# Blocks 3 to 5 in 64-token chunks, q scaled while it is turned, y copied by two engines, and a new order of the work

## The chip, the cores and the metric

One core of one Trainium2 chip runs the whole program. The metric is the device time of one execution in microseconds (us), the median of several runs; lower is better. Engines are named as in the profile: PE is TensorE (matmuls; PEld its weight loads), DVE is VectorE, ACT is ScalarE, POOL is GpSimd, SP is SyncE. PSUM has eight banks, numbered 0 to 7.

## The reference

Two layers follow each other: a retention with a decay per head, then a channel mix.

```python
# B=4, H=8, S=768, D=64
for t in range(S):
    state = gamma[h] * state + outer(k[:, :, t], v[:, :, t])
    y[:, :, t] = (1 / sqrt(D)) * q[:, :, t] @ state
x = y.transpose(0, 2, 1, 3).reshape(B, S, 512)
xk = mu_k * x + (1 - mu_k) * x_prev        # x_prev: x one token earlier
xr = mu_r * x + (1 - mu_r) * x_prev
k = relu(xk @ w_k)                          # 512 -> 1024
out = sigmoid(xr @ w_r) * (k * k @ w_v)     # 512 x 512, 1024 -> 512
```

## The kernel before, in words

The tokens are cut into twelve blocks of 256, three for each batch element; block n holds tokens of batch n // 3. The recurrence is done in chunks: within a chunk the scores of q and k are multiplied by a causal mask and then by v, and what went before comes in through a 64x64 state for each head, which is summed from chunk to chunk. The decay is taken out of the scores by scaling: v is multiplied by powers of gamma when it is cast (`vs`), and y by the opposite powers when it leaves PSUM (`gy`).

A block can take one of three forms. Blocks 6 to 11 (`HALF`) use chunks of 64 tokens and matmuls of 64x64 tiles. Blocks 2 to 5 (`WIDE`) use chunks of 128 tokens, with wider tiles. Blocks 0 and 1 use 128-token chunks in four quarters. `PAIRQ` and `PAIRK` name the blocks whose q or k is laid out so that two heads are turned (transposed) by one 128x128 product; the others in `HALF` are turned in 64x64 quarters. Blocks 9 to 11 are turned by DMA.

After its y is in `xT`, a block goes through the channel mix: the difference to the token before (`dx`), xk and xr (`X`), the product with w_k (`K`), relu and square, the product with w_r (`R`), the sigmoid, the product with w_v (`V`), the product of both and the store. Blocks 3 and 4, 6 and 7, 9 and 10 share `dx`, `X` and `K`.

Nothing is scheduled by a compiler: the string `ORDER` lists every step, and each engine gets its instructions in that order. A word such as `K.2.0@3` is a code, its arguments (block, part) and the PSUM banks; `~a`, `~v`, `~p`, `~s` choose ScalarE, VectorE, GpSimd's queue or SyncE's queue. The codes used below are:

- `lq`, `lk`, `lv`: loads of a block, issued by POOL; `st`: store of a result, by SP; `tq`, `tk`: turn of q or k by DMA, by SP
- `Tq`, `Tk`: turn by PE into PSUM; `Eq`, `Ek`: the copy of it to `qT`, `kT` by ACT
- `vs`: v scaled and cast, by DVE; `S`: scores (PE); `M`: mask (DVE, PSUM to `a`)
- `C`: k times v, the state of each chunk (PE); `U`: its running sum (DVE or ACT, into `tg`, at the end `t`); `G`: the decay to the next block, into `tg`
- `I`: the part of y from the states that goes to the other chunk half (PE, first into y's two banks); `Y`: scores times v, and in `HALF` blocks also the rest of the state part; `J`: that rest in `WIDE` blocks; `D`: y from PSUM to `xT`
- `dx`, `X`, `K`, `Qa` (relu, into `kr`), `Qb` (square, into `k2s`), `R`, `s` (sigmoid, into `rs`), `V`, `O` (the result, `os`)
- `z`: matmuls on zeros, early in the program

Rings of buffers bind the order: four each for q, k, v as loaded and for `kr`, three each for `vs`, `qT`, `kT` and `a`.

Of the kernel before, what the change touches and what calls it, by code (L numbers as in the profile page):

```python
# [37 lines left out]
z.2@5 Y.1 lv.2~p X.0.0.1 X.0.0.2 z.1@5 K.0.2@4 Tk.2@5 D.1~v X.0.1.0 dx.1~v Qa.0.2 X.0.1.2
X.1.0.0 Ek.2~a K.0.3@0 Qa.0.3 Qb.0.3 X.1.0.2 X.1.0.1 S.2.1@67 K.0.0@5 Qa.0.0 K.0.1@0 X.1.0.3
K.1.2@1 K.1.0@5 Qb.0.0 wr~p X.1.1.0 Qa.0.1 U.1.1 G.1~a vs.2~v X.0.1.3 Qa.1.0 Qa.1.2 Qb.0.1  # L40
X.1.1.1 C.2@0 U.2.0 K.1.1@3 Qa.1.1 I.2@45 lv.3~p M.2.1~v S.2.0@01 K.1.3@2 lq.3~p Qb.1.2 R.0.1@3
Qa.1.3 lk.3~p M.2.0~v X.1.1.2 Y.2 lk.4~p lq.4~p Qb.1.3 s.0.1 lv.4~p X.1.1.3 vs.3~v J.2 D.2~v
R.1.0@2 R.1.1@3 Qb.1.1 s.1.0 Tq.3@2 s.1.1 Eq.3~a C.3@67 Tk.3@4 Ek.3~a R.0.0@3 s.0.0 Tk.4@2
S.3.0@01 wv.0~p dx.2~v X.2.0.0 X.2.0.2 X.2.0.1 X.2.0.3 X.2.1.1 S.3.1@45 Ek.4~a K.2.0@3 lq.7~p
Tq.4@2 M.3.1~v U.3.0~a U.3.1 Qa.2.0 wv.1~p Eq.4~a K.2.3@6 Qa.2.3 M.3.0~v K.2.1@7 S.4.1@45
S.4.0@23 vs.4~v M.4.0~v K.2.2@6 Qb.0.2 I.3@01 Y.3 C.4@23 G.3~a M.4.1~v U.4.0 lk.5~p Qb.1.0
Qa.2.2 V.1.0.0@6 lq.5~p I.4@45 Qa.2.1 Qb.2.1 X.2.1.3 J.3 D.3~v Y.4 V.0.1.0@7 V.0.0.0@0 J.4 U.4.1
Tq.7@23 Eq.7~a V.1.1.0@1 V.1.1.1 G.4~a Qb.2.0 dx.3~v V.0.0.1 Tk.5@2 Ek.5~a D.4~v dx.4~v V.0.1.1
Qb.2.3 V.1.0.1 Tq.5@2 X.3.0.3 X.3.0.1 X.3.0.2 Eq.5~a X.3.0.0 K.3.1@3 Qa.3.1 K.3.3@4 O.1.1 O.0.0
S.5.0@01 O.1.0 O.0.1 lv.5~p lq.6~p M.5.0~v S.5.1@23 vs.5~v K.3.2@5 Qa.3.3 lk.6~p Qb.3.3 K.3.5@4  # L50
M.5.1~v X.2.1.0 Qa.3.2 X.2.1.2 Tq.6@67 Qa.3.5 Tk.6@01 Eq.6~a lv.6~p lv.7~p Ek.6~a C.5@5 U.5.0
X.3.1.0 Qb.3.1 K.3.0@4 Qa.3.0 lk.7~p K.3.7@6 S.6@23 Qb.3.2 M.6~v I.5@01 Y.5 vs.6~v V.2.1.0@7
R.2.1@2 lv.10~p Qb.2.2 Qa.3.7 K.3.4@6 st.0.0 vs.7~v Qb.3.7 s.2.1 st.0.1 V.2.1.1 Tk.7@45 Qb.3.5
Qa.3.4 X.3.1.3 X.3.1.1 Qb.3.0 C.6@23 st.1.0 J.5 Ek.7~a X.3.1.2 R.2.0@6 lv.8~p U.6.0~a D.5~v
U.6.1 U.6.2 U.6.3 V.2.0.0@4 s.2.0 K.3.6@6 dx.5~v Qa.3.6 lq.8~p lk.8~p st.1.1 R.4.1@5 I.6@01
# [24 lines left out]
R.11.1@0 V.11.0.0@7 R.11.0@4 O.9.0 st.9.0 V.11.0.1 O.10.1 s.11.1 st.10.1 s.11.0 O.10.0 st.10.0  # L80
O.11.0 st.11.0 Vc.11.1.0@4 Oc.11.1.0 sc.11.1.0~s Vc.11.1.1@6 Oc.11.1.1 sc.11.1.1~a
"""


# [1 line left out]
def kernel(  # L86
# [210 lines left out]
    def trans(a):
        def go(e, n, j0=0, j1=NJ):
            src = held_as(n, a)
            pt = turned(n, a, j0, j1)  # L300
            for j in range(j0, j1):
                for i in range(2):
                    if quarters(n, a):
                        for u in range(2):
                            for s, h, hp in heads(j):
                                nc.tensor.transpose(  # L306
                                    pt[low(s), u, j - j0, i], src[low(u), i, h], ident[low(u), low(u)]
                                )
                        continue
# [256 lines left out]

    def yout(e, n, u=None):
        x, c = col(n)
        if half(n):
            x = x[:, :, c : c + TM].rearrange("p j (i u t) -> p j i u t", i=2, u=2)  # L570
            g = gy.rearrange("p j (i u t) -> p j i u t", i=2, u=2)
            for v in range(2):
                nc.vector.tensor_tensor(
                    out=x[:, :, :, v],
                    in0=banks("I", n)[:, v].rearrange("p (j i t) -> p j i t", j=NJ, i=2),
                    in1=g[:, :, :, v], op=ALU.mult,
                )
            return
# [88 lines left out]
        nc.scalar.activation(out=kr, in_=banks("K", n, g, *u), func=AF.Relu)  # L667
# [143 lines left out]
    def load_wv(e, h):  # L811
# [62 lines left out]
```

## Time and profile before

| | us |
|---|---|
| median of 3 runs | 154.3 |
| lowest and highest run | 154.3, 154.64 |
| span of the profiled execution | 152.4 |
| PE busy | 145.3 |
| DVE busy | 128.0 |
| ACT busy | 94.5 |
| POOL busy | 62.1 |

The span runs from the first to the last instruction of the profiled execution; a run's time also has what lies around it, here 1.9 us between the span and the median. Busy shares are of the span: 95% for PE, 84% for DVE, 62% for ACT. The granted clock of PE was 1.0 throughout. PE's busy time alone does not say that PE is at its peak, since matmuls are pipelined; so the places where it waits, and the start times of its groups, are what is read.

### The profile page before, as it was taken

The numbers are of one execution on the slowest core, as the hardware profiler recorded it, in microseconds if no ns is written. First come the engines' busy times: TensorE is split into PE (matmuls) and PEld (weight loads), VectorE is DVE, ScalarE is ACT, GpSimd is POOL, SyncE is SP. The second block draws the span as 40 slices with busy tenths as digits, with TensorE's granted clock in tenths as the row PEclk, the third lists the DMA queues.
The fourth block names the chain that finished last, engine by engine and source line by source line (L and its number), as shares of the span: only waits on it lengthen the run. The fifth ranks groups of instructions, "written<-read, shape, count | busy, mean of one in ns | idle before, by whom it ended". The sixth has DMA issues, their size and how long they took to land.

```text
span 152.4 us, 4956 instructions
## 1 busy us (share of the span) xinstructions
PE 145.3 (95%) x2129; PEld 82.4 (54%) x2129; DVE 128.0 (84%) x204; ACT 94.5 (62%) x172; POOL 62.1 (41%) x77
## 2 busy tenths in 40 slices
PE   7969899999999999999999999999999999999991
PEld 3345467657864545545448544447664444466460
DVE  2289999999999999999999998998999999331651
ACT  3655259979955679966418807869450089739430
POOL 7965658999746920599989000000000000000000
PEclk9999999999999999999999999999999999999999
DMA  5999999999999999299999999928103013003153
GB/s 146 237 241 192 181 240 237 148 148 223 167 178 216 213 225 286 68 239 166 258 188 238 236 168 126 152 89 109 38 4 138 0 71 142 0 0 138 69 207 138
DMA packets 56525, 23.83 MB, mean 156 GB/s; under 512 B 48056, under 2 KB 52024, under 8 KB 56504
## 3 DMA queue, kind: packets, MB, share of 16 engines
q0 software_dynamic: 45200, 14.95, 82.1%
q1 hardware_dynamic: 10872, 8.26, 22.3%
q8 instruction: 16, 0.26, 0.7%
q10 hardware_dynamic: 432, 0.32, 0.7%
q14 instruction: 5, 0.04, 0.1%
HBM read 24.31 MB, written 6.29 MB: 201 GB/s over the span
## 4 chain that ended last, share of the span: by engine, by line
PE 73%; DVE 11%; DMA 11%; issue 2%; ACT 0%; DVEq 0%; POOLq 0%
PE ps L700 24%; PE ps L688 14%; PE ps L635 12%; PE ps L645 11%; DMA kT<-k 6%; DMA v<-in_v_dram 5%; DVE a L420 3%; PE ps L507 2%; PE ps L311 2%; DVE xk L621 2%; DVE xT L580 2%; DVE dx L595 2%; PE ps L544 1%; DVE vs L280 1%; PE ps L388 1%
## 5 line engine op out<-in xcount | busy, mean ns | idle before, releaser
L700 PE MATMUL ps<-wv,k2s 128*128 128x512 f16 x184 | 43.9, 380 | 0.0
L667 ACT ACTIVATE kr<-ps 128x512 f32<-128x512 f32 x48 | 27.9, 594 | 23.0 <-PE ps L635 14.9
L700 PEld LDWEIGHTS <-k2s 128*128 128x128 f16 x184 | 17.2, 98 | 19.0
L706 DVE SCALAR_TENSOR_TENSOR os<-ps,rs 128x512 f32<-128x512 f32 x23 | 15.2, 684 | 12.1 <-PE ps L700 6.5
L688 PE MATMUL ps<-wr,xr 128*128 128x512 f16 x96 | 24.0, 379 | 0.0
L259 POOL DMA_DIRECT2D v<-in_v_dram x20 | 18.0, 911 | 13.6 <-DVE vs L280 8.3
L645 PE MATMUL ps<-xk,wk 128*128 128x256 f16 x192 | 23.4, 273 | 0.0
L635 PE MATMUL ps<-xk,wk 128*128 128x512 f16 x96 | 22.8, 379 | 0.0
L420 DVE TENSOR_TENSOR a<-ps,c_sb 128x1024 f16<-128x1024 f32 (+1 forms) x20 | 21.9, 1110 | 0.0
L694 ACT ACTIVATE rs<-ps 128x512 f32<-128x512 f32 x24 | 14.3, 594 | 10.6 <-PE ps L688 8.8
L645 PEld LDWEIGHTS <-wk 128*128 128x128 f16 x192 | 18.2, 98 | 3.9
L621 DVE SCALAR_TENSOR_TENSOR xr<-dx,mu,xT 128x256 f16<-128x256 f32 (+1 forms) x36 | 19.3, 566 | 0.0
L621 DVE SCALAR_TENSOR_TENSOR xk<-dx,mu,xT 128x256 f16<-128x256 f32 (+1 forms) x36 | 18.9, 569 | 0.3
L259 POOL DMA_DIRECT2D k<-in_k_dram x20 | 17.7, 896 | 3.5 <-DMA wv<-in_moe_w_v_dram 1.6
L280 DVE TENSOR_TENSOR vs<-v,csm_sb 128x1024 f16<-128x1024 f32 x12 | 14.5, 1217 | 3.3 <-DMA v<-in_v_dram 3.3
L675 ACT ACTIVATE k2s<-kr 128x512 f16<-128x512 f32 x24 | 14.7, 626 | 0.4
L595 DVE TENSOR_TENSOR dx<-xT 128x1024 f32<-128x1024 f32 x12 | 14.6, 1221 | 0.2
L635 PEld LDWEIGHTS <-wk 128*128 128x128 f16 x96 | 9.1, 98 | 10.5 <-issue 0.2
L679 ACT ACTIVATE k2s<-kr 128x512 f16<-128x512 f32 x24 | 14.5, 625 | 0.3
L688 PEld LDWEIGHTS <-xr 128*128 128x128 f16 x96 | 9.0, 98 | 10.0
L265 ACT COPY qT<-ps 128x1024 f16<-128x1024 f16 (+1 forms) x10 | 9.2, 924 | 7.7 <-PE ps L317 3.7
L265 ACT COPY kT<-ps 128x1024 f16<-128x1024 f16 (+1 forms) x10 | 9.3, 934 | 6.9 <-PE ps L306 3.4
(73 smaller groups left out, 151.3 us busy)
## 6 DMA issues: line engine op xcount, KB each, us to landing
out_dram<-os SPq DMA_DIRECT2D x23, 256.0 KB, 3.8
v<-in_v_dram POOLq DMA_DIRECT2D x20, 256.0 KB, 6.8
k<-in_k_dram POOLq DMA_DIRECT2D x21, 128.0 KB, 6.9
q<-in_q_dram POOLq DMA_DIRECT2D x13, 128.0 KB, 7.1
q<-in_q_dram POOLq DMA_DIRECT2D x5, 256.0 KB, 9.0
v<-in_v_dram POOLq DMA_DIRECT2D x2, 512.0 KB, 7.3
wv<-in_moe_w_v_dram POOLq DMA_DIRECT2D x2, 512.0 KB, 9.5
wk<-in_moe_w_k_dram POOLq DMA_DIRECT2D x2, 256.0 KB, 9.6
```

The costliest lines, as they stand in the source:

```text
L259: e.dma_start(out=to[:, i, hs], in_=src[:, i])
L265: e.copy(out=out, in_=in_)
L280: e.tensor_tensor(out=VS(n), in0=V32(n).rearrange("p (h i d) -> p i h d", i=2, h=H), in1=gks[:, int(half(n) or wide(n)), :, :, None].to_br ...
L420: nc.vector.tensor_tensor(out=dst, in0=dst if n in SPLITM else src, in1=mask[:, None, None, :].to_broadcast(list(dst.shape)), op=ALU.mult,)
L595: e.tensor_tensor(out=DX(k)[:, :, m * TM + t0 : m * TM + t1], in0=x[:, :, c + t0 : c + t1], in1=x[:, :, c - 1 + t0 : c - 1 + t1], op=ALU.s ...
L621: nc.vector.scalar_tensor_tensor(out=XM[w](k)[:, j, t0:t1], in0=DX(k)[:, j, t0:t1], scalar=mu[:, w * NCO + j : w * NCO + j + 1], in1=x[:, ...
L635: nc.tensor.matmul(banks("K", n, g), lhsT=wk16[:, co, g * P : g * P + P], rhs=XM[0](k)[:, co, :], start=(co == 0), stop=(co == NCO - 1),)
L645: nc.tensor.matmul(pz[:, i, :], lhsT=wk16[:, co, fo * P : fo * P + P], rhs=XM[0](k)[:, co, m * TM + t0 : m * TM + t1], start=(i == 0 and c ...
L667: nc.scalar.activation(out=kr, in_=banks("K", n, g, *u), func=AF.Relu)
L688: nc.tensor.matmul(banks("R", n, tb), lhsT=XM[1](k)[:, co, t : t + P], rhs=wr16[:, co, :], start=(co == 0), stop=(co == NCO - 1),)
L700: nc.tensor.matmul(banks("V", n, tb), lhsT=K2(n)[:, fo, tb * P : tb * P + P], rhs=wv16[:, fo, :], start=(fo == 0), stop=(fo == NFO - 1),)
L706: nc.vector.scalar_tensor_tensor(out=OS(2 * n + tb), in0=banks("V", n, tb), scalar=1.0 / (KSC * KSC), in1=RS(2 * n + tb), op0=ALU.mult, op ...
```

## The change

The blocks 3, 4 and 5 leave `WIDE` and the pair layouts and join `HALF`: their q and k are turned in 64x64 quarters, and scores, states and y are computed in chunks of 64 tokens. That changes their instructions: one mask of 1024 columns in place of two, four running sums in place of two (three in place of one in block 5, whose last sum isn't needed).

For blocks 3 to 8 the turn of q is no longer a transposition by an identity but a product with a scaled identity, `turn`, which has the power of gamma for each token and head. Its result is float32 in two banks, where it was float16. Their y then needs one constant factor alone, so `D` becomes a scaled copy instead of a product with `gy`; it can run on ACT, and does for blocks 4, 6 and 8 (`D.4~a`, `D.6~a`, `D.8~a`). The scaled identity is built once by two DVE instructions (`tu`) from a small table `late` that SP loads (`ce`) into the tile `mu8`, after `mt` has read that tile; it lies in the unused half of the first `a` buffer.

A new step `sy` (`settle`) makes ACT read a few elements of y's banks after `I` and before `Y`, in blocks 2, 3, 4, 5, 7, 10 and 11. `Y` on PE then waits for that read. The two banks of each two-bank tile are neighbours. The whole `ORDER` is written anew.

```diff
-HALF = (6, 7, 8, 9, 10, 11)
+QDN = 64.0
+HALF = (3, 4, 5, 6, 7, 8, 9, 10, 11)
-PAIRQ = (3, 4, 5, 9, 10, 11)
-PAIRK = (3, 4, 5, 9, 10, 11)
-WIDE = (2, 3, 4, 5)
+PAIRQ = (9, 10, 11)
+PAIRK = (9, 10, 11)
+WIDE = (2,)
+QS = (3, 4, 5, 6, 7, 8)
...
-M.0.1.2.4~v I.0@01 mt@2 me lq.1~p S.0.0.2.4@67 M.0.0.2.4~v lq.2~p G.0~a
+I.0@01 mt@2 M.0.1.2.4 S.0.0.2.4@67 me ce~s G.0~a
...
+    late = mu8[:, 0 : 2 * H + W]
+    turn = A2(0)[:, 2 * H * W :].rearrange("p (i h t) -> p i h t", i=2, h=H)
...
+    def load_late(e):
+        e.dma_start(out=late, in_=lated.ap())
+    def scaled_eye(e, h0, h1):
+        hs = slice(h0, h1)
+        gq = late[:, 0 : 2 * H].rearrange("p (i h) -> p i h", i=2)
+        to = [P, 2, h1 - h0, W]
+        e.tensor_tensor(
+            out=turn[:, :, hs], in0=late[:, None, None, 2 * H :].to_broadcast(to),
+            in1=gq[:, :, hs, None].to_broadcast(to), op=ALU.mult,
+        )
...
+                                if scaled(n, a):
+                                    nc.tensor.matmul(
+                                        pt[low(s), u, j - j0, i], lhsT=src[low(u), i, h],
+                                        rhs=turn[low(u), i, h], start=(j == j0 and i == 0),
+                                        stop=(j == j1 - 1 and i == 1), skip_group_check=True,
+                                    )
+                                    continue
...
+    def settle(e, n):
+        if wide(n):
+            u = slice(1 if first(n) else 0, 2)
+            copy(e, seen_y[:, u], banks("I", n)[:, u, 0 : NJ * C : C])
+        else:
+            copy(e, seen_y[low(0), 0, 0:2], banks("I", n)[low(0), 0, NJ * C - 2 :])
...
+        if n in QS:
+            x = x[:, :, c : c + TM].rearrange("p j (i u t) -> p u j i t", i=2, u=2)
+            y = banks("I", n).rearrange("p u (j i t) -> p u j i t", j=NJ, i=2)
+            for v in range(2):
+                if e is nc.scalar:
+                    e.activation(
+                        out=x[:, v], in_=y[:, v], func=AF.Copy, scale=0.125 * KSC / KUP * QDN
+                    )
+                else:
+                    e.tensor_scalar(
+                        out=x[:, v], in0=y[:, v], scalar1=0.125 * KSC / KUP * QDN, scalar2=None,
+                        op0=ALU.mult,
+                    )
+            return
```

Three places in the order of instructions follow. The first is on VectorE, early in the program: from y of block 0 (`xT` from `ps`) over its `dx` and first `X` (`xk`, `xr`) to the sum and the masks of block 1. Before:

```order
L580 TENSOR_TENSOR xT_130<-ps,gy_sb 128x2x4x128
L595 TENSOR_TENSOR dx_99<-xT_130 128x4x256
L621 SCALAR_TENSOR_TENSOR xk_101<-dx_99,mu,xT_130 128x256
L621 SCALAR_TENSOR_TENSOR xr_104<-dx_99,mu,xT_130 128x256
L485 TENSOR_TENSOR tg_1_94<-ps,tg_1_88 128x256
L420 TENSOR_TENSOR a_1_84<-ps,c_sb 128x1024 x2
L621 SCALAR_TENSOR_TENSOR xk_101<-dx_99,mu,xT_130 128x256 x3
```

And now:

```order
L640 TENSOR_TENSOR xT_130<-ps,gy_sb 128x2x4x128
L655 TENSOR_TENSOR dx_99<-xT_130 128x4x256
L681 SCALAR_TENSOR_TENSOR xk_101<-dx_99,mu,xT_130 128x256
L310 TENSOR_TENSOR a_0_83<-mu_124 128x2x256 x2
L681 SCALAR_TENSOR_TENSOR xr_104<-dx_99,mu,xT_130 128x256
L522 TENSOR_TENSOR tg_1_94<-ps,tg_1_88 128x256
L457 TENSOR_TENSOR a_1_84<-ps,c_sb 128x1024 x2
L681 SCALAR_TENSOR_TENSOR xk_101<-dx_99,mu,xT_130 128x256 x3
```

The two instructions that build `turn` (written into `a_0` from the tile of mu) have come between two `X`; the rest stands as before.

The second place is on ScalarE around the decay of block 3 (`G.3`, four instructions into `tg_1_88`), with the copies of q (`qT`), relus (`kr`), squares (`k2s`) and a sigmoid (`rs`) ahead of it. Before:

```order
L265 CAST tg_0_93<-ps 128x256
L667 ACTIVATE kr_109<-ps 128x512
L265 COPY qT_78<-ps 128x1024
L667 ACTIVATE kr_110<-ps 128x512
L679 ACTIVATE k2s<-kr_107 128x512
L490 ACTIVATE tg_1_88<-t_0_86,csm_sb 128x64 x4
L679 ACTIVATE k2s<-kr_108 128x512
```

And now:

```order
L276 CAST qT_78<-ps 128x2x4x128
L745 ACTIVATE k2s<-kr_108 128x512
L276 CAST tg_0_90<-ps 128x256
L745 ACTIVATE k2s<-kr_109 128x512
L760 ACTIVATE rs_112<-ps 128x512
L727 ACTIVATE kr_110<-ps 128x512
L727 ACTIVATE kr_107<-ps 128x512
L727 ACTIVATE kr_108<-ps 128x512
L527 ACTIVATE tg_1_88<-t_0_86,csm_sb 128x64 x4
L276 COPY seen_y<-ps 64x2
```

The read `sy.3` (`seen_y`) stands behind `G.3`, and more relus stand ahead of `G.3` than before.

The third place is on SyncE's queue, where the turns by DMA for blocks 9 to 11 stand among the stores. Before:

```order
L713 DMA out_dram<-os_116 128x512
L351 DMA_TRANSPOSE qT_78<-q_2_64 128x8x128
L713 DMA out_dram<-os_118 128x512
L351 DMA_TRANSPOSE kT_81<-k_2_68 128x8x128
L351 DMA_TRANSPOSE kT_80<-k_1_67 128x8x128
L351 DMA_TRANSPOSE qT_77<-q_1_63 128x8x128
L351 DMA_TRANSPOSE qT_79<-q_3_65 128x8x128
```

And now:

```order
L779 DMA out_dram<-os_118 128x512
L388 DMA_TRANSPOSE kT_81<-k_2_68 128x8x128
L779 DMA out_dram<-os_119 128x512
L388 DMA_TRANSPOSE qT_78<-q_2_64 128x8x128
L779 DMA out_dram<-os_118 128x512
L388 DMA_TRANSPOSE qT_77<-q_1_63 128x8x128
L388 DMA_TRANSPOSE kT_80<-k_1_67 128x8x128
```

Of block 10 the k (`kT_81`) is now turned first and the q (`qT_78`) behind it and a store, where q came first.

More of the change, by code (lines that the diff above doesn't have):

```diff
@@ L38 @@
[L38 to L43, printed above, removed]
@@ L80 @@
[L80 to L81 removed]
+lq.0.0.2~s lk.0.0.2~s lv.0~p mu~s lk.0.2.4~p gy.0~v lq.0.2.4~p lv.1~p cq.0.0.2~a lk.1~p z.8@7
+Tq.0.0.2@0 ck.0.0.2~a lq.1~p Eq.0.0.2~a lq.2~p z.3@7 Tk.0.0.2@0 Ek.0.0.2~a wk.1~p gy.1~a z.3@7
+S.0.0.0.2@01 S.0.1.0.2@23 vs.0~v Tk.0.2.4@4 Ek.0.2.4~a M.0.1.0.2 C.0@67 lk.2~p Tq.0.2.4@5 U.0.0~v
+M.0.0.0.2 Eq.0.2.4~a U.0.1 z.3@4 S.0.1.2.4@45 I.0@01 mt@2 M.0.1.2.4 S.0.0.2.4@67 me ce~s G.0~a
@@ new lines @@
+M.0.0.2.4 vs.1~v wk.0~p z.4@3 Y.0 Tk.1@6 D.0~v Ek.1~a z.3@5 Tq.1@7 dx.0~v C.1@01 Eq.1~a X.0.0.0
+tu.0.4~v z.4@5 S.1.1@67 lv.2~p tu.4.8~v X.0.1.1 U.1.0~v M.1.1 wr~p z.1@4 I.1@45 S.1.0@23 M.1.0
+Tq.2@6 Eq.2~a X.0.0.3 z.2@7 Y.1 X.0.0.1 X.0.0.2 Tk.2@6 D.1~v K.0.2@7 Ek.2~a lv.3~p K.0.3@2 X.0.1.2
+Qa.0.2~a U.1.1 dx.1~v K.0.1@3 lq.3~p S.2.0@01 X.0.1.3 Qa.0.1~a S.2.1@67 X.1.0.1 K.0.0@4 Qa.0.3~a
+X.1.0.2 Qb.0.1~a X.1.0.0 lk.3~p X.1.0.3 G.1~a X.0.1.0 K.1.1@5 X.1.1.1 Qb.0.3~a M.2.1 K.1.0@2
+Qa.1.1~a lk.4~p R.0.1@3 Qb.1.1~a vs.2~v Qa.0.0~a K.1.3@5 Qa.1.0~a lq.4~p M.2.0 s.0.1 C.2@2
@@ new lines @@
+sy.5~a st.1.1 M.5 st.1.0 Qa.3.3~a K.3.1@2 lv.10~p Qb.3.3~a X.3.1.1 K.3.6@1 Qb.3.4~a vs.7~v
+Qa.3.7~a S.7@67 Qa.3.1~a Y.5 lk.8~p R.3.0@0 Qb.3.1~a D.5~v Qb.3.2~a R.3.1@2 Qb.3.0~a lq.9~p M.7
+K.3.5@3 s.3.1 s.3.0 dx.5~v V.3.0.0@4 Qb.3.7~a lq.10~p R.4.1@0 Qa.3.5~a X.5.0.1 Qa.3.6~a X.5.1.0
+C.6@23 Qb.3.5~a X.5.0.3 Tk.6@67 X.5.0.2 R.4.0@1 U.6.0~a Qb.3.6~a U.6.1 X.5.1.2 Ek.6~a V.4.0.0@5
+X.5.0.0 X.5.1.1 V.3.0.1 s.4.1 U.6.2 s.4.0 U.6.3 S.6@67 X.5.1.3 G.6~a I.6@23 C.7@01 O.3.0 V.4.0.1
+lk.11~p M.6 K.5.0@4 U.7.0~v K.5.1@6 U.7.1 lk.10~p Qa.5.0~a U.7.2 K.5.2@7 U.7.3 Qa.5.1~a O.4.0
@@ new lines @@
+V.8.1.0@6 V.7.0.0@7 dx.9~v V.8.0.0@0 D.10~v V.7.1.0@1 V.7.0.1 dx.10~v R.7.0@2 R.8.1@3 X.9.0.1
+s.7.0 X.9.0.0 Qb.8.2~a V.7.1.1 s.8.1 X.9.0.3 V.8.1.1 X.9.0.2 V.8.0.1 G.10~v O.7.1 K.9.1@3 O.7.0
+st.7.1 X.9.1.0 K.9.4@1 st.7.0 Qa.9.1~a st.6.1 X.9.1.1 K.9.0@7 X.9.1.2 K.9.6@3 O.8.0 Qa.9.0~a
+Qa.9.4~a X.9.1.3 K.9.2@2 U.11.0~v K.9.3@7 U.11.1 Qa.9.2~a O.8.1 Qb.9.4~a R.10.1@1 U.11.2 st.8.1
+Qa.9.3~a R.9.0@6 Qb.9.0~a Qb.9.3~a K.9.7@7 Qa.9.6~a Qb.9.2~a S.11@45 I.11@23 s.10.1 K.9.5@0 M.11
+sy.11~a Qb.9.1~a R.9.1@1 Qa.9.5~a Qa.9.7~a V.10.1.0@4 Qb.9.6~a s.9.0 Y.11 V.9.0.0@0 Qb.9.5~a
@@ L82 @@
+D.11~v Qb.9.7~a R.10.0@5 s.9.1 dx.11~v V.9.1.0@2 V.9.0.1 X.11.0.3 X.11.1.1 V.10.1.1 X.11.0.1
+X.11.0.0 V.9.1.1 X.11.0.2 K.11.0@1 O.9.1 K.11.3@3 X.11.1.3 st.9.1 Qa.11.0~a O.10.1 K.11.1@2
+X.11.1.0 Qa.11.3~a st.10.1 X.11.1.2 V.10.0.0@4 O.9.0 Qa.11.1~a st.9.0 R.11.0@0 Qb.11.1~a st.8.0
+Qb.11.0~a K.11.2@1 s.10.0 V.11.0.0@2 Qa.11.2~a Qb.11.3~a V.10.0.1 Qb.11.2~a R.11.1@1 O.10.0
+V.11.0.1 st.10.0 s.11.1 s.11.0 Vc.11.1.1@3 O.11.0 Vc.11.1.0@0 Oc.11.1.1 st.11.0 sc.11.1.1~a
+Oc.11.1.0 sc.11.1.0~s
 """
@@ L138 @@
     ).astype(np.float32)
+    gq_np = gam[None, None, :] ** (toks[0][:, :, None] + 1 - TM) / QDN
+    late_np = np.concatenate(
+        [gq_np.reshape(P, -1), np.tile(np.eye(W), (2, 1))], axis=1
+    ).astype(np.float32)
+    lated = nc.inline_tensor(late_np, name="late")
     c16d = nc.inline_tensor(c16_np, name="c16")
@@ L286, in quarters, with scaled @@
         return half(n) and n not in PAIR[a]
+    def scaled(n, a):
+        return a == 0 and n in QS
+    def load_late(e):
[8 more added lines that the diff above has]
+        )
     def turned(n, a, j0, j1):
+        if scaled(n, a):
+            pt = banks("T", n, a, j0)
+            return pt.rearrange("c u (j i p) -> c u j i p", j=NJ, i=2)[:, :, j0:j1]
         pt = banks("T", n, a, j0).bitcast(F16)
@@ L305, in go @@
                             for s, h, hp in heads(j):
+                                if scaled(n, a):
+                                    nc.tensor.matmul(
[4 more added lines that the diff above has]
+                                    continue
                                 nc.tensor.transpose(
@@ L520, in inter_on @@
         inter(n, 0)
+    seen_y = const.tile([P, 2, NJ], F32, name="seen_y")
+    def settle(e, n):
[4 more added lines that the diff above has]
+            copy(e, seen_y[low(0), 0, 0:2], banks("I", n)[low(0), 0, NJ * C - 2 :])
     def intra_half(n):
@@ L669, in squared @@
     def squared(e, n, g, *u):
+        if e is nc.gpsimd:
+            kr = held.pop((n, g, u))
+            idle.append(kr)
+            to = k2s[:, n % 3 : n % 3 + 2, g, :] if joint(n) else K2(n)[:, 2 * g : 2 * g + 2]
+            e.tensor_tensor(out=to, in0=kr, in1=kr, op=ALU.mult)
+            return
         w = 4 if u else 2
```

68 lines of the change are left out of this document (25 added, 43 removed).

## The prediction

> **What bounds the kernel now.** I read the stretches of the span first: busy time of each engine by stage.
>
> ```profile
> 8.30:27.70 19.40, 17.62 (x351) 11.63 (x351) 19.14 (x30) 11.15 (x24) 13.08 (x17) 1.00 1.46 212
> 27.70:60.00 32.30, 32.24 (x498) 19.94 (x500) 31.87 (x45) 25.63 (x46) 21.83 (x26) 1.00 1.67 199
> 60.00:90.00 30.00, 30.00 (x542) 16.64 (x539) 29.42 (x47) 18.81 (x35) 20.28 (x23) 1.00 1.51 196
> 90.00:120.00 30.00, 29.57 (x502) 16.25 (x500) 28.25 (x43) 16.27 (x29) 0.00 (x0) 1.00 0.61 94
> 120.00:149.10 29.10, 29.03 (x204) 15.40 (x202) 16.93 (x32) 18.06 (x32) 0.00 (x0) 1.00 0.23 84
> 149.10:152.40 3.30, 0.00 (x0) 0.00 (x0) 0.40 (x1) 0.00 (x0) 0.00 (x0) 1.00 0.40 140
> ```
>
> The columns are length, then PE, PEld, DVE, ACT, POOL busy, then clock and DMA. From 8.3 to 27.7 us DVE is full (19.14 of 19.40) and PE fills its gaps with matmuls on zeros: the start is DVE's. From 27.7 to 149.1 us PE is idle for 0.56 us of 121.4; it is the bound, and DVE, though nearly as full until 120, is waited for almost nowhere. So two things move the end: PE's work after 27.7 us, and the moment at which DVE lets PE run full. The last 3.3 us are the last result and its store, and the change leaves them.
>
> **PE's work.** The before has both forms side by side, blocks 3 to 5 wide and 6 to 8 in halves, so the price of the new form needs no guess. In the timeline of PE (start, busy, line, operation, tile, count) the price of a group is the next group's start less its own.
>
> ```profile
> 31.39 0.64 PE L544 MATMUL ps<-a,vs 128*64 128x128 f16 x16
> 31.96 0.31 PE L507 MATMUL ps<-qT,tg 64*64 64x128 f16 x8
> 32.20 1.90 PE L688 MATMUL ps<-wr,xr 128*128 128x512 f16 x8
> ...
> 34.48 0.44 PE L450 MATMUL ps<-vs,k 128*64 128x64 f16 x16
> 34.85 0.62 PE L311 MATMUL ps<-c_sb,k 128*128 128x128 f16 x8
> ...
> 36.17 0.61 PE L311 MATMUL ps<-c_sb,k 128*128 128x128 f16 x8
> 36.71 0.62 PE L388 MATMUL ps<-qT,kT 64*128 64x128 f16 x16
> 37.27 1.05 PE L645 MATMUL ps<-xk,wk 128*128 128x256 f16 x8
> ...
> 56.75 0.45 PE L306 MATMUL ps<-c_sb,q 64*64 64x64 f16 x32
> 57.02 0.44 PE L306 MATMUL ps<-c_sb,k 64*64 64x64 f16 x32
> ...
> 64.36 0.44 PE L432 MATMUL ps<-vs,k 64*64 64x64 f16 x32
> 64.62 0.32 PE L507 MATMUL ps<-qT,tg 64*64 64x128 f16 x8
> ...
> 70.86 0.45 PE L375 MATMUL ps<-qT,kT 64*64 64x64 f16 x32
> 71.11 0.45 PE L528 MATMUL ps<-a,vs 64*64 64x64 f16 x32
> 71.39 0.32 PE L507 MATMUL ps<-qT,tg 64*64 64x64 f16 x12
> ```
>
> - Scores: wide 36.71 to 37.27, 0.56 us; halves 70.86 to 71.11, 0.25. Three blocks save 0.9.
> - Scores times v: wide 31.39 to 31.96, 0.57; halves 71.11 to 71.39, 0.28. Three blocks save 0.9.
> - Turns of q and k: pairs 36.17 to 36.71, 0.54; quarters 56.75 to 57.02, 0.27. Six turns would save 1.6; a pair's 0.54 has part of a switch in it, so I take 1.3.
> - States: 0.37 (34.48 to 34.85) against 0.26 (64.36 to 64.62): 0.2 for blocks 3 and 4, nothing for block 5.
> - State part of y: two groups of 0.24 (31.96 to 32.20) a block against two shorter ones; see the switch below. I take 0.1 a block, 0.3.
>
> The scaled turn is the same 32 products of 64x64 with another moving operand, so I cost it like the quarters it replaces; its float32 result is bounded by 0 and 0.1 us for each of six blocks, and I take 0, as a score group writes float32 into two banks in 0.25. The sum is 3.6 us less work for PE.
>
> What a change of tile shape costs is seen where the same 16 products stand ahead of the same small shape or of a full 128x128 one:
>
> ```profile
> 78.66 0.32 PE L507 MATMUL ps<-qT,tg 64*64 64x64 f16 x16
> 78.81 0.44 PE L306 MATMUL ps<-c_sb,k 64*64 64x64 f16 x32
> ...
> 89.40 0.32 PE L507 MATMUL ps<-qT,tg 64*64 64x64 f16 x16
> 89.65 1.04 PE L700 MATMUL ps<-wv,k2s 128*128 128x512 f16 x4
> ```
>
> 0.15 against 0.25: a switch back to the full array costs 0.10 us. Counted in the two orders from the first `K` on, PE returns to the full array 25 times before and 20 times now, which is another 0.5 us less; I count 0.3, since part stands in the turns already. The Trainium skill (TensorEngine Tiling (Array Packing), Key Properties) says that changing the tiling mode drains TensorE, which would speak against turns that leave the full array; the rows agree that there is a drain, at 0.1 us. PE's total is 3.9 us less.
>
> **DVE's start.** The two `tu` are 512 columns each between two `X`. The nearest row is a mask of 512 columns, and the path that they push back ends in block 2's `xk`:
>
> ```profile
> 9.44 0.69 DVE L420 TENSOR_TENSOR a<-ps,c_sb 128x512 f16<-128x512 f32 x1
> 10.09 0.42 DVE L267 CAST tg<-ps 128x256 f16<-128x256 f32 x1
> ...
> 11.42 0.19 PE L764 MATMUL ps<-csm_sb,mu 8*128 8x8 f32 x1
> ...
> 16.75 0.48 DVE L621 SCALAR_TENSOR_TENSOR xr<-dx,mu,xT 128x256 f16<-128x256 f32 x1
> ...
> 32.94 1.22 DVE L580 TENSOR_TENSOR xT<-ps,gy_sb 128x1024 f32<-128x1024 f32 x1
> 34.19 1.23 DVE L595 TENSOR_TENSOR dx<-xT 128x1024 f32<-128x1024 f32 x1
> 35.45 1.67 DVE L621 SCALAR_TENSOR_TENSOR xk<-dx,mu,xT 128x256 f16<-128x256 f32 x4
> ```
>
> Two times 0.6 (0.65 from 9.44 to 10.09) is 1.2 us. Between them and y of block 2 DVE does the same set of instructions as before, without idle time. So y of block 2 moves from 32.94 to 34.1 us, and its four `xk` end at 38.2 instead of 37.0. PE has `K.2` directly behind; in the new order the work left to it up to there (three `R`, `K.1`, turns of blocks 3 and 4, scores of 3) ends near 37.8, so it stalls about 0.5 us and starts `K.2` at 38.3. The bounds are 0 and 1.2.
>
> The table `late` is loaded behind the turn of mu at 11.42 and needed at 16.75, where the next `X` began. The constants, of the same 40 KB, landed in 2.2 us with the DMA nearly free; turned q took 9.2 with it full. I take 3 to 4 us, in time; the far bound would hold DVE 3.9 us (20.6 against 16.75). The rows are DMA issues, with KB and us to landing, and the one wait of PE for such a turn:
>
> ```profile
> csm_sb<-csmall ACTq DMA_DIRECT2D x1, 40.0 KB, 2.2
> qT<-q SPq DMA_TRANSPOSE x3, 9.2
> ```
>
> ```profile
> 95.42 0.45 PE L375 MATMUL ps<-qT,kT 64*64 64x64 f16 x32 [0.43 <-DMA kT<-k]
> ```
>
> **The other edits on DVE and ACT.** Three masks go, six sums come, three y leave DVE (groups, with count, busy and mean ns; then ACT's timeline):
>
> ```profile
> L420 DVE TENSOR_TENSOR a<-ps,c_sb 128x1024 f16<-128x1024 f32 x16 | 19.2, 1217 | 0.0
> L485 DVE TENSOR_TENSOR tg<-ps,tg 128x256 f16<-128x256 f32 x20 | 8.4, 420 | 0.6 <-PE ps L432 0.3
> ```
>
> ```profile
> 40.81 1.06 ACT L490 ACTIVATE tg<-t,csm_sb 128x64 f16<-128x64 f32 x4
> 41.76 0.63 ACT L679 ACTIVATE k2s<-kr 128x512 f16<-128x512 f32 x1
> 42.28 1.08 ACT L667 ACTIVATE kr<-ps 128x512 f32<-128x512 f32 x2
> ```
>
> Three masks of 1.2 are 3.6 less, six sums 6 x 0.42 = 2.5 more, three y leave with 1.2 (block 4, wide) and twice 2 x 0.69 (512 columns, as the mask at 9.44), 4.0 less, and the two `tu` add 1.2: DVE has about 4 us less. PE does not wait for DVE after the start, so this buys room and no time; it is also the cover for all of DVE's moved instructions, and without it DVE (29.42 of 30 in the stage from 60) would be the next to be waited for. On ACT the three y add six copies of about 0.5 (relus of the same size, two in 1.08), 3 us on 94.5, which its idle time from 60 us on takes.
>
> The seven `sy` are small, but `Y` waits for them, and all that stands behind `Y` on PE waits too. I went through each with the two queues. For blocks 4, 5, 7, 10 and 11 ACT has nothing unfinished ahead of the read by the time `I` ends, and one or more groups stand between `I` and `Y`; nothing is lost. For block 2 the read comes 0.15 late. For block 3 it stands behind `G.3`, which needs the last sum of block 3. An instruction of DVE overlaps the next by some 0.08 (four `xk` take 1.67, one 0.48). After the `xk` at 38.2 come an `X` (0.4), the mask (1.13), two sums (0.7), `vs` (1.13) and the third sum (0.34): 41.9. Three relus on ACT end at 42.1; `G.3` takes 0.95 (40.81 to 41.76) and the read 0.15, so `Y.3` starts at 43.3. PE comes to it at 42.6: from 38.3 four `K.2` of 0.9 (half as many columns as the eight `R` in 1.90 at 32.20), then the state part, the states and the scores of block 4. It waits 0.65 us.
>
> **The sum.** Work 3.9 less. The new order has paid 1.2 us at DVE, which `K.2` shows as 0.5 of stall and the rest as gaps before it, 0.8 in the waits of `Y.2` and `Y.3`, and 0.4 for the last terms: the scores of block 10, for which PE already waits 0.43, come up to 0.5 us before q's turn has landed, now the second in the queue. 3.9 - 1.2 - 0.8 - 0.4 = 1.5 us. The profiled span goes from 152.4 to 150.9; with the 1.9 us around it the median goes from 154.3 to **152.8 us**.
>
> **The rivals.**
>
> (a) *All of it shows.* PE banks enough work before `K.2` and the waits for `sy` vanish. For it: PE was idle for only 0.56 us before, with waits as tight. Against it: DVE is full from 8.3 us, so 1.2 us must go somewhere. 154.3 - 3.9 + 0.6 = 151.0 us. Chance 0.18.
>
> (b) *Slower: the read becomes PE's bound.* The place is `Y` of blocks 2, 3, 4, 7 and 10, where only 0.3 to 0.7 us of PE work stands between `I` and `Y`. If ACT, in order, is two instructions of 0.5 late at each (its copies of float32 turns or its strided y slower than I price them), each costs 1.0 less some 0.4 of cover, 0.6; four of these and block 3 at 2 us lose 4.4 against the 0.8 counted: 152.8 + 3.6 = 156.4. It decides from 1.5 us of such waits more than I count; at half of it the time is 154.6. Chance 0.2.
>
> (c) *Slower: the DMA for blocks 9 to 11.* On SP k's turn of block 10 waits for a load that POOL now issues last of all k loads, and stores and three turns queue behind it. At 9.2 us from issue to landing for the second, the scores of block 10 come 3 us late and PE with them: 152.8 + 2.5 = 155.3. For it: the one stall of PE in the row at 95.42. Against it: only two loads of v stand behind that load on POOL, so the turns have less traffic beside them. Chance 0.09.
>
> (d) *It does little*: `late` lands 1.5 us late and DVE's start costs 2.7: 152.8 + 1.5 = 154.3. Chance 0.1.
>
> **How the numbers follow.** The forecast has 0.43, its own range 152.0 to 153.6 from the bounds of the turns, the stall at `K.2` and the wait of block 3. A measurement of this kernel tells 0.3%, 0.46 us, from no change: 153.84 to 154.76 is the same. The forecast and (a) are faster, 0.61; of (b) 0.12 lies above 154.76, 0.05 is the same and 0.03 below; of (d) 0.06 is the same and 0.02 on either side; (c) is slower. That makes faster 0.66, same 0.11, slower 0.23. The range leaves out the lower half of (a), 0.09, and the upper half of (b), 0.1, and takes in (c): 151.0 to 155.3.
>
> **What would show it.** Right: PE's groups of 32 products in blocks 3 to 5 at 0.25 to 0.28; the two `tu` at 0.6 from 16.7 us on, with no wait for DMA; `K.2` starting about 38.3; waits of PE under 0.8 at `Y.2` and `Y.3`; PE ending near 147.6. Wrong: PE waiting for ACT's reads at more than two blocks, DVE waiting for `late`, or PE idle for over 3 us after `K.2`.

## The result: slower by 3.5%

| | before | after |
|---|---|---|
| median | 154.3 us (4 runs, 154.04 to 154.64) | 159.81 us (4 runs, 159.43 to 161.84) |
| ratio, 95% interval | | 1.0348 (1.0312 to 1.0384) |
| span of the profiled execution | 152.4 us | 158.1 us (time 159.94) |
| PE busy | 145.3 us, 2129 matmuls | 143.8 us, 2464 matmuls |

Ratios, here and below, are of runs in the chip's faster state alone, while medians take in every run.

The forecast was 152.8 us, with 155.3 as its upper end: it has the wrong sign. PE has less to do, as foreseen, and ends 5.9 us later (154.96 us instead of 149.03).

The stretches of the span of the changed kernel, in the columns of the prediction's first view:

```profile
8.30:29.00 20.70, 17.68 (x359) 12.03 (x360) 20.21 (x32) 11.31 (x24) 15.47 (x20) 1.00 1.46 209
29.00:60.00 31.00, 26.94 (x592) 16.57 (x591) 25.70 (x40) 21.74 (x44) 16.52 (x19) 0.94 1.46 205
60.00:90.00 30.00, 27.62 (x643) 15.89 (x642) 25.33 (x41) 21.42 (x40) 20.23 (x23) 1.00 1.45 155
90.00:120.00 30.00, 30.00 (x558) 16.65 (x556) 27.01 (x44) 19.52 (x37) 0.00 (x0) 1.00 0.63 131
120.00:155.00 35.00, 34.96 (x276) 18.24 (x274) 23.84 (x40) 17.83 (x34) 0.00 (x0) 1.00 0.18 69
```

From 29 to 90 us PE is idle for 6.4 of 61 us, where before it was idle for 0.1 of 62; from 90 us on it is full again. No other engine is full there: DVE has 25.70 of 31 and 25.33 of 30 us, where before it had 31.87 of 32.3 and 29.42 of 30. The waits of PE (what it waited for, us in total, times, longest):

```profile
PE ps L337 <- issue: 2.0, 1, 2.0
...
PE ps L574 <- issue: 1.2, 1, 1.2
...
PE ps L766 <- issue: 0.8, 1, 0.8
PE ps L705 <- issue: 0.7, 1, 0.7
PE ps L574 <- ACT seen_y L276: 0.6, 1, 0.6
...
PE ps L469 <- DMA k<-in_k_dram: 0.5, 1, 0.5
```

Four of them, 4.79 us together, have no releaser: "issue" is time in which the engine waited for nothing that the profile shows. The largest, in the timeline of PE:

```profile
37.11 0.45 PE L412 MATMUL ps<-qT,kT 64*64 64x64 f16 x32
37.38 0.23 PE L337 MATMUL ps<-a,q 64*64 64x64 f16 x5
39.64 0.59 PE L337 MATMUL ps<-a,q 64*64 64x64 f16 x27 [2.04 <-issue]
39.99 0.66 PE L469 MATMUL ps<-vs,k 64*64 64x64 f16 x32
```

PE stops after 5 of the 32 products of one turn. The 6th is of the same group, reads the same tiles and writes the same two banks, and the trace shows no semaphore that it waited for. What the four places have in common is their count. In PE's records (matmuls, weight loads and, up to there, six semaphore instructions and the like), in order of start and counted from 0, they stand at numbers 1217, 1985, 2497 and 3265, all 193 plus a multiple of 256. And one DMA queue of the profile fits that step: it carries packets of 16 KB, or 64 bytes for each of 256 instructions, and there are 19 of them for 4928 recorded matmuls and weight loads after, 16 for 4258 before. After, then before:

```profile
q8 instruction: 19, 0.31, 0.8%
```

```profile
q8 instruction: 16, 0.26, 0.7%
```

Set beside the times of those packets (worked out from the records of the trace; from here on a page is a stretch of 256 instructions of PE):

```
after: page begun | its last instruction | packet from..to | PE goes on, in the next page
       33.09      | 37.41                | 37.23..38.21   | 39.64
       53.78      | 58.34                | 57.11..58.11   | 59.55
       66.58      | 70.39                | 69.56..70.51   | 71.82
       85.19      | 88.57                | 86.68..88.08   | 89.52
```

At these four the packet starts 1.5 to 4.1 us after PE has begun the page, and PE goes on 1.3 to 1.4 us after it has landed. From the start of a page to the point where the next can begin it took 6.55, 5.77, 5.25 and 4.33 us here; PE had used the page up in 4.3, 4.6, 3.8 and 3.4. In before, with the boundaries at the same numbers, the shortest page while loads ran lasted 5.08 us and no boundary has a pause. The theory (F) is then: the smaller tiles do the same work with more instructions (4928 in place of 4258), 32 products of 64x64 are 64 instructions in 0.27 us, and where pages are used up faster than they are brought, PE stands still.

### The profile page after: what moved, and what is told of

It reads as the page before. It is cut to its first block, busy times and chain, and to the rows that moved or that the text cites. A ratio compares the mean times of both kernels' runs of the same rounds, so it can differ in the third digit from the quotient of the medians.

```text
span 158.1 us, 5629 instructions
## 1 busy us (share of the span) xinstructions
PE 143.8 (91%) x2464; PEld 82.0 (52%) x2464; DVE 125.0 (79%) x206; ACT 96.3 (61%) x185; POOL 59.4 (38%) x74
## 4 chain that ended last, share of the span: by engine, by line
PE 57%; DVE 11%; issue 11%; DMA 10%; POOL 7%; ACT 1%; DVEq 0%; POOLq 0%
PE ps L766 18%; PE ps L754 10%; PE ps L695 9%; PE ps L705 7%; DMA k<-in_k_dram 6%; DMA v<-in_v_dram 4%; POOL v L270 3%; POOL k L270 3%; DVE a L457 3%; DVE vs L291 2%; DVE xk L681 2%; PE ps L544 2%; PE ps L840 1%; DVE xr L681 1%; PE ps L469 1%
## 5 line engine op out<-in xcount | busy, mean ns | idle before, releaser
L705 PE MATMUL ps<-xk,wk 128*128 128x256 f16 x192 | 24.3, 281 | 1.2 <-issue 0.7
L457 DVE TENSOR_TENSOR a<-ps,c_sb 128x1024 f16<-128x1024 f32 (+1 forms) x17 | 18.4, 1093 | 5.1 <-PE ps L412 3.7
L695 PE MATMUL ps<-xk,wk 128*128 128x512 f16 x96 | 22.2, 379 | 0.0
L705 PEld LDWEIGHTS <-wk 128*128 128x128 f16 x192 | 19.0, 101 | 6.0 <-issue 1.5
L772 DVE SCALAR_TENSOR_TENSOR os<-ps,rs 128x512 f32<-128x512 f32 x23 | 15.7, 686 | 7.7 <-PE ps L766 5.6
L681 DVE SCALAR_TENSOR_TENSOR xr<-dx,mu,xT 128x256 f16<-128x256 f32 (+1 forms) x36 | 19.9, 566 | 0.0
L291 DVE TENSOR_TENSOR vs<-v,csm_sb 128x1024 f16<-128x1024 f32 x12 | 14.6, 1217 | 3.3 <-DMA v<-in_v_dram 3.3
L695 PEld LDWEIGHTS <-wk 128*128 128x128 f16 x96 | 9.1, 98 | 10.7
L522 DVE TENSOR_TENSOR tg<-ps,tg 128x256 f16<-128x256 f32 x26 | 10.9, 420 | 4.4 <-ACT tg L276 2.6
```

Of the source, the lines that this page charges most:

```text
L291: e.tensor_tensor(out=VS(n), in0=V32(n).rearrange("p (h i d) -> p i h d", i=2, h=H), in1=gks[:, int(half(n) or wide(n)), :, :, None].to_br ...
L457: nc.vector.tensor_tensor(out=dst, in0=dst if n in SPLITM else src, in1=mask[:, None, None, :].to_broadcast(list(dst.shape)), op=ALU.mult,)
L681: nc.vector.scalar_tensor_tensor(out=XM[w](k)[:, j, t0:t1], in0=DX(k)[:, j, t0:t1], scalar=mu[:, w * NCO + j : w * NCO + j + 1], in1=x[:, ...
L695: nc.tensor.matmul(banks("K", n, g), lhsT=wk16[:, co, g * P : g * P + P], rhs=XM[0](k)[:, co, :], start=(co == 0), stop=(co == NCO - 1),)
L705: nc.tensor.matmul(pz[:, i, :], lhsT=wk16[:, co, fo * P : fo * P + P], rhs=XM[0](k)[:, co, m * TM + t0 : m * TM + t1], start=(i == 0 and c ...
L772: nc.vector.scalar_tensor_tensor(out=OS(2 * n + tb), in0=banks("V", n, tb), scalar=1.0 / (KSC * KSC), in1=RS(2 * n + tb), op0=ALU.mult, op ...
```

## Experiments

### Boundaries moved by 16 and by 52 small matmuls

The rivals to F: the pauses belong to the instructions at which they stand (the scaled turn, above all), or to the loads alone. In the first two kernels 16, or 52, matmuls of 64x64 on zeros are added in the start, where PE has time; each is two instructions, so every later boundary falls 32, or 104, instructions earlier in the work.

```diff
- z.1@4 I.1@45
+ z.1@4 pd.16@4 I.1@45        # e1_shift32;  pd.52 in e2_shift104
+    for x in range(count):
+        nc.tensor.matmul(pz[low(x % 2), 0:D], lhsT=z16[low(1), 0:D], rhs=z16[low(1), 0:D], start=True, stop=True, ...)
```

> The changed kernel with 16 tiny matmuls on zeros added to PE early, at 17 us, where PE sat idle for 1.55 us; nothing else changes. Theory F (instructions arrive in pages of 256, and PE stalls where it uses up a page sooner than 4.3 to 6.5 us after it began it): the 32 added instructions move every page boundary 32 instructions earlier in the program. The four stalls at 37.6, 58.7, 70.6 and 88.8 us leave their places; the two longest are now in front of the scores times v of block 4 (near 54 us, 3 to 4.5 us) and near 88 us (2 to 3 us). Time 161 to 164 us against 159.8. Theory Q (something in the instructions themselves, such as the scaled turn of block 4, stops PE): the stalls stay at the same instructions, 159.8 within 0.5.

> The same with 52 tiny matmuls, so boundaries move by 104 instructions. Theory F: stalls near 36, 47 (about 2 us) and 81 us, none at 58.7, 70.6 and 88.8; sum of the stalls 1.5 us less, time 157.5 to 159.5. Theory Q: same places, 159.8 within 0.5.

Measured: 169.33 us, ratio 1.1004 (1.0959 to 1.1048), with 16; 167.06 us, 1.0844 (1.0797 to 1.0891), with 52. None of the four pauses stays at its instruction; all stand again at 193 plus a multiple of 256, those of the first kernel now in other steps:

```profile
PE ps L754 <- issue: 3.6, 1, 3.6
PE ps L544 <- issue: 2.9, 1, 2.9
...
PE ps L412 <- issue: 1.6, 1, 1.6
PE ps L469 <- issue: 1.2, 1, 1.2
```

The largest has a page begun at 53.53 us and used up at 54.77: two state groups of 16, 64 scaled products and 32 scores times v stood in one page, the packet came from 56.06 to 57.35, and PE went on at 58.79. In the first kernel place and direction were as F said, though its time was too short by over 5 us. In the second, the three places that F had named pause (pages used up at 36.8, 48.5 and 85.9 us), but three more do so too, and the kernel is slower than the changed one where F had it faster: a miss by 7.6 us. F's times had been worked out with the delays of the one trace of after, and what follows a pause (below) was not in them.

### The same without the loads, and without the scaled turns

```diff
- lk.5~p ... lq.5~p ... lv.11~p     # e3_no_loads: no load of q, k, v of blocks 5 to 11
```

```diff
- QS = (3, 4, 5, 6, 7, 8)           # e4_unscaled: q turned unscaled, into float16, y scaled by gy
+ QS = ()
- tu.0.4~v ... tu.4.8~v
```

> The changed kernel with the loads of q, k and v of blocks 5 to 11 left out (those blocks compute on what the buffers hold), so that DMA has little to do after 45 us. Theory F with a page's way lengthened by the loads that it queues behind: the stall at 37.6 stays near 2 us, the stalls at 58.7, 70.6 and 88.8 together fall from 2.75 us to under 1, and the wait for k at 77.3 goes: 156 to 157 us. If a page takes as long without the loads: 159.3. If the stalls are ACT's or DVE's: 159.3.

> The changed kernel with q of blocks 3 to 8 turned by plain transpositions again (float16 result), y multiplied by the powers on DVE as before, the scaled identity not built; PE has the same number of instructions. Theory F: the same four stalls at the same instructions, 4 to 5 us together; the start is 1.3 us earlier: 158.5 to 160. Theory Q (scaled turn, float32 result): the stall in the turn of block 4 goes, and time falls to about 157.

Without the loads (blocks 5 to 11 work on what the buffers hold): 155.33 us, 1.0121 (1.0047 to 1.0195). All waits of PE of 0.2 us and more from 25 us on (a line of PE has here a number lower by 51, so L286 is the turn at L337 above):

```profile
PE ps L286 <- issue: 1.6, 1, 1.6
PE ps L523 <- ACT seen_y L225: 0.6, 1, 0.6
PE ps L493 <- DVE tg L471: 0.4, 1, 0.4
```

The pause near 40 us stays, since the earlier loads still run there. Of the other three only 0.1 us is left (at 84.94); the two of them that had paused longest end pages that are used up in the same 4.6 and 3.8 us as in after, but the packets now begin before the page or within a microsecond of its start, where it had been 3.0 and 3.3 us. The loads are what delays the packets; the smaller tiles are what makes the delay matter.

Without the scaled turns: 158.71 us, 1.0211 (1.0139 to 1.0282). The time decides nothing: the ratio stands for some 157 us, which is the rival's figure. The trace decides. The four boundaries pause at the same numbers, now with a plain transpose at the first (1.76, 1.19, 0.14 and 1.70 us; the smallest is not in the view):

```profile
PE ps L343 <- issue: 1.8, 1, 1.8
PE ps L705 <- issue: 1.7, 1, 1.7
PE ps L766 <- issue: 1.2, 1, 1.2
```

So the scaled turn is not the cause of the pauses. (The profiled run, 160.22 us, is the longest of four from 156.41 on; only the presence of the pauses is read from it.) No kernel without the reads `sy` was run; in no trace did a group of PE wait longer than 0.6 us for one of them.

A control for the loads: before, with the same loads left out.

> The kernel before without the loads of blocks 5 to 11 (their q, k and v are what the buffers hold), as e3_no_loads did with the changed kernel. Theory F (loads only delay the bringing of instructions, and before has no such stall): only the wait of 0.43 us for k's turn can go: 153 to 154.5 us. Rival L (the loads slow any kernel by their traffic, so that what e3_no_loads gained, about 4.5 us, says nothing of instructions): 149.5 to 151 us.

Measured: 153.21 us, 0.9936 (0.9904 to 0.9967). The loads are worth 1.1 us to before and 4.5 to after (1.0 and 3.5 by the ratios): rival L falls.

### Before, with its boundaries moved

If F holds, the kernel before must be slowed by added matmuls in one place and not in another, without any part of the change.

```diff
- z.1@0 I.1@01
+ z.1@0 pd.8@0 I.1@01         # e6a_before_shift16;  pd.56 in e6b_before_shift112
```

> The kernel before with 8 small 64x64 matmuls on zeros added in its head, where PE is idle for DVE: every later boundary of 256 PE instructions comes 16 instructions earlier, and nothing else changes. Theory F (PE stops where it uses up a stretch of 256 instructions faster than the next is brought): the shortest stretches stay at 4.65, 4.8 and 5.1 us, as long as before, so no stall: 153.5 to 154.5 us. Rival P (added matmuls cost by themselves, 16 of them had cost 9.5 us in the changed kernel): 8 of them cost 4 to 5 us, 158 to 159 us.

> The kernel before with 56 such matmuls: boundaries 112 instructions earlier. By the starts in the trace of before a stretch of 256 instructions is then used up in 2.2 us, from 78.8 to 81.0 us, all others in 4.8 or more. Theory F: one stall of 2 to 4 us near 81 us inside a group, with no releaser, and 0 to 1.7 us of half clock behind it: 156.3 to 159 us, in a kernel without any part of the change. Rival P: seven times the cost of the run with 8; rival C (the stalls belong to the new tiles, banks or settle reads of the change): no stall, 154 us.

Measured: 154.26 us, 1.0017 (0.9989 to 1.0046), with 8; 160.6 us, 1.0373 (1.0324 to 1.0421), with 56. The second is as slow as the changed kernel. With 8 the trace shows only one short stop at a boundary, 0.34 us from start to start at 21.64. The same steps in the timeline of PE, with 8:

```profile
79.63 0.42 PE L306 MATMUL ps<-c_sb,q 64*64 64x64 f16 x30
79.87 0.45 PE L528 MATMUL ps<-a,vs 64*64 64x64 f16 x32
80.14 0.35 PE L507 MATMUL ps<-qT,tg 64*64 64x64 f16 x16
80.42 3.67 PE L645 MATMUL ps<-xk,wk 128*128 128x256 f16 x32
```

and with 56:

```profile
82.33 0.44 PE L306 MATMUL ps<-c_sb,k 64*64 64x64 f16 x32
...
84.18 0.45 PE L528 MATMUL ps<-a,vs 64*64 64x64 f16 x32
84.45 0.28 PE L507 MATMUL ps<-qT,tg 64*64 64x64 f16 x7
87.00 0.27 PE L507 MATMUL ps<-qT,tg 64*64 64x64 f16 x9 [2.26 <-issue]
87.19 5.01 PE L645 MATMUL ps<-xk,wk 128*128 128x256 f16 x29
```

The page that F had named from the trace of before (used up in 2.2 us) is begun at 82.33 and ends after 7 of 16 products at 84.54; its packet lands at 85.57, and PE goes on 1.43 us later. Rivals P (added matmuls cost by themselves) and C (the new tiles, banks or reads cause it) both fall. The time is 1.6 us above F's bound, because the 56 matmuls also filled a page of the start, which F had left out: a second pause of 2.29 us at 22.47. Behind each of the two, 3.4 us of half clock: 29 products of K take 5.01 us there, 32 take 3.67 above.

### Fewer instructions

```diff
- PAIRQ = (9, 10, 11)
+ PAIRQ = (3, 4, 5, 6, 7, 8, 9, 10, 11)   # e8_qpairs, from e4_unscaled; e9 adds pd.52@4
- PAIRK = (9, 10, 11)
+ PAIRK = (3, 4, 5, 6, 7, 8, 9, 10, 11)   # e7_kpairs, from the changed kernel
```

> The changed kernel without the scaled turns (as in e4_unscaled), and with q of blocks 3 to 8 turned as pairs, 8 products of 128x128 in place of 32 of 64x64: 288 fewer PE instructions, and 6 x 0.27 = 1.6 us more work for PE. Theory F: the stalls near 59.6 and 89.3 us go, some 1.3 us near 39 and 0.6 near 85 stay: 155 to 157 us, faster than the 158.7 of e4_unscaled although PE works longer. Rival W (PE's work and waits set the time, instruction count does not): 158.7 + 1.6 = 160.3 us.

> The same with 52 small matmuls on zeros in the head, which puts the boundaries where the stretches of 256 instructions last longest. Theory F: one stall of 0.6 us or less, 154.5 to 156 us, not slower than e8_qpairs and nearly the time of before. Rival P (added matmuls cost by themselves): 160 us or more.

> The changed kernel with its scaled turns of q kept, and k of blocks 3 to 8 turned as pairs: 288 fewer PE instructions, 6 x 0.27 = 1.6 us more work for PE. Theory F: of the four stalls (4.8 us) some 0.5 us near 39 and 0.6 near 82 stay, and the half clock behind the first goes: 156 to 157.5 us. Rival W (PE's work sets the time, the number of instructions does not): 159.8 + 1.6 = 161.4 us.

Measured: e8_qpairs 156.53 us, 1.0131 (1.0089 to 1.0173); e9_qpairs_shift104 161.52 us, 1.0414 (1.0347 to 1.0481); e7_kpairs 161.57 us, 1.0486 (1.0436 to 1.0536). In e8_qpairs two pauses are left, at 44.45 and 75.87 us, other places than F's arithmetic had, with other waits between, so that its time lies in F's range partly by luck:

```profile
PE ps L469 <- DMA k<-in_k_dram: 0.8, 1, 0.8
PE ps L574 <- issue: 0.7, 1, 0.7
PE ps L574 <- ACT seen_y L276: 0.6, 1, 0.6
PE ps L766 <- issue: 0.4, 1, 0.4
```

Rival W had 1.6 us more than e4_unscaled, a ratio of about 1.031; the whole interval lies below. That e8_qpairs is faster than e4_unscaled is likely, but their intervals overlap. The other two missed F's times. Their traces show F's mechanism with pages that F's arithmetic had not put there: in e9_qpairs_shift104 a page of the start used up in 3.6 us (pause 2.06 us) and one at 75.88 in 3.8 (1.79 us), beside 1.2 us of waiting for k and 1.0 for a sum; in e7_kpairs one at 82.90 used up in 2.2 us (pause 2.19 us, then half clock) and two smaller ones near 39 and 46 (1.1 us). By their times alone e7_kpairs would fit W, and e9_qpairs_shift104 would fit P (160 us or more), so these two decide nothing; against P stands the kernel before with 8 matmuls. What decides is not how many instructions there are in all, but where a boundary falls among the dense groups: removing 288 of them moves every later boundary too. None of these kernels beats before, and the runs point to no version that would without another order of PE's groups.

### All boundaries together

In the twelve traces (before, after and the ten kernels above) PE stopped over 0.25 us, from one start to the next, at 30 page boundaries after the first 14 us. At every one it went on 1.21 to 1.65 us after the packet had landed. From the start of a page to that point it took 3.8 us (e3_no_loads, at 81 us) to 6.9 us, once 8.2. Pages that were used up in 3 us without a pause begin after 95 us, when loads are nearly over. That the pauses come from the supply of instructions rests on this, on e1, e2, e6a and e6b; that loads lengthen its delay rests on e3 and e10. How the packet is ordered among the loads, and why 1.4 us pass after it has landed, stays open.

The Trainium skill (Runtime: NRT & Kernel Launch, Instruction fetch mechanics) describes this supply: each engine's sequencer fetches the next block of 256 instructions by its own DMA queue while the present one runs, and crossing a boundary is "mostly hidden". The blocks agree. That it is hidden holds for before and not for after, where it costs 4.79 us.

## Why the prediction was wrong, step by step

**The step that failed** is "So two things move the end: PE's work after 27.7 us, and the moment at which DVE lets PE run full." There is a third, the rate at which PE gets its instructions. Before was never slowed by it, so its trace has no pause to price, and the sum had no term and no rival for it. Two things could have raised the question: the queue "q8 instruction" in the profile of before, whose 16 packets answer to boundaries from 11 to 128 us, 7.8 us for a page on average, with a shortest of 5.08 under loads; and PE's count of instructions in the new order, which rises by 670 while the work falls. What was read from the orders were prices of groups, not how many instructions a microsecond holds. "PE idle for over 3 us after K.2" stood in the list of what would make the forecast wrong; it was 4.0 us.

**PE's work** was over-sized: 3.9 us forecast, 2.2 measured. The prices of single groups were right (start, busy, line; 0.27 and 0.26 from start to start):

```profile
66.48 0.45 PE L343 MATMUL ps<-c_sb,k 64*64 64x64 f16 x32
66.75 0.44 PE L412 MATMUL ps<-qT,kT 64*64 64x64 f16 x32
67.01 0.35 PE L544 MATMUL ps<-qT,tg 64*64 64x64 f16 x16
```

But they were taken where one small group stands behind another. Over all groups from the first K on, start to start without pauses of over 0.1 us, 32 scores cost 0.32, 32 turns 0.34, and 32 scores times v 0.30 us, since many stand ahead of a full-array group. So scores saved 0.74 instead of 0.9, scores times v 0.58 instead of 0.9, turns 0.8 instead of 1.3, states and their part of y 0.1 instead of 0.5; the 0.3 for switches is not there beside these. The total of such times falls from 126.6 to 124.4 us (without the half clock's 1.2, and without a turn of 0.6 us that stands ahead of the first K only in the new order).

**DVE's start** went as forecast. DVE's timeline:

```profile
16.55 1.29 DVE L310 TENSOR_TENSOR a<-mu 128x512 f16<-128x512 f32 x2 [0.16 <-DMA mu<-late]
...
34.11 1.22 DVE L640 TENSOR_TENSOR xT<-ps,gy_sb 128x1024 f32<-128x1024 f32 x1
35.37 1.22 DVE L655 TENSOR_TENSOR dx<-xT 128x1024 f32<-128x1024 f32 x1
36.63 1.67 DVE L681 SCALAR_TENSOR_TENSOR xk<-dx,mu,xT 128x256 f16<-128x256 f32 x4
```

The two `tu` took 1.29 us for 1.2, `late` was 0.16 us late, y of block 2 came at 34.11 for 34.1, and its `xk` ended near 38.2. `K.2` started at 40.59, which less the pause of 2.04 us is 38.55 for 38.3; part of the rest is the half clock, under which the two groups ahead ran. Rival (d) had no part in it.

**The waits for `sy`** went as forecast too: 0.61 us at `Y.3` for 0.65, nothing at `Y.2` for 0.15, none elsewhere. Rival (b), the slower side of the forecast, named the wrong mechanism. The scores of block 10 did not wait (0.4 forecast), so (c) fell as well; instead PE waited 0.46 us at 77.30 for k of block 6, whose load stands behind that of block 9 on POOL, a place that the prediction had not followed.

**The sum again.** From the forecast's -1.5 us: work +1.7, pauses +4.8, wait for k +0.5, half clock +1.2, `K.2` +0.2, the terms that did not come -0.6: +6.3 us, against 5.7 measured between the two spans. Why the terms come to 0.6 too much stays open. The half clock is worth less than its term, by two other runs of after with a mean clock of 1.0: their spans are 157.9 and 157.7 us, only 0.2 to 0.4 less. Their pauses were not recorded. Without pauses, half clock and that wait, these terms leave the change a gain of 0.2 us: 1.5 - 1.7 - 0.2 + 0.6.

## What to carry to other kernels

The smaller tiles saved array time here and were paid for in instructions. So beside the work of a PE-bound kernel, count the instructions of each stretch of 256, and set the time in which it is used up against the time in which the trace shows the next being brought (here 4 to 6.5 us while loads run). Idle time of PE inside a group of like matmuls, put down to "issue", at equal distances in the count of instructions, is this limit; adding a few idle instructions ahead moves it, and so tests it. A gain of some 2% in such a kernel can turn on where the boundaries fall. An order that is tuned by hand or by a planner might therefore spread its dense groups among long ones; no run here tests such an order.

## What the runs showed of the hardware

- Behind a pause the clock can halve. In before the granted clock stays at 1.0 to the end of PE's work. In after it was 0.5 from 39.44 to 42.85 us, behind the pause of 2.04; the 32 products of `K.2` took 4.75 us in place of 3.6 to 3.7:

```profile
40.59 4.75 PE L705 MATMUL ps<-xk,wk 128*128 128x256 f16 x32
```

  It came for 3.4 us or twice that, in e1_shift32 for 6.8 us behind 3.64 us of idle time. The stretch behind the pause of e6b_before_shift112, with 0.66 as its clock:

```profile
87.00:92.00 5.00, 5.00 (x38) 3.83 (x38) 4.51 (x7) 1.54 (x3) 0.47 (x1) 0.66 2.03 221
```

  The Trainium skill (TensorE: Matmul & The Clock Gate, Why this matters for your kernels) says to keep idle gaps of PE under about 3 us; here shorter ones were enough. In the twelve traces all eight gaps of PE of 2.04 us and more were followed by half clock. Of eleven gaps from 1.3 to 1.8 us five were, among them 1.31 (e1_shift32, at 18.85) and 1.76 (e4_unscaled, at 39.04), and six were not, among them 1.59 (e3_no_loads, at 40.07) and 1.79 (e9_qpairs_shift104, at 81.69). So the length of the gap alone does not decide it in that range; what does was not tested.
- Eight small matmuls in the start cost nothing that can be measured, 56 cost 6 us: the price lies in the place of the boundaries, not in the matmuls.
- A packet of instructions took 0.9 to 1.7 us once it ran; what varies more is when it starts, from before PE reached the page to 5.6 us behind.
